# Linear attention into a two-layer ELU network on one core: a first load on another queue, a merged key-value product, and the stores of the last block

## The chip, the core and the metric

The kernel runs on one core of a Trainium2 chip. A core has five engines that run their own instruction streams and meet at semaphores: TensorE (PE, matrix products; its weight loads are shown apart as PEld), VectorE (DVE), ScalarE (ACT), GpSimd (POOL) and SyncE (SP). SP, ACT and POOL also start DMA transfers, each through a queue of its own. TensorE writes to PSUM, here eight banks of 128 x 512 floats, from where VectorE and ScalarE fetch results.

The metric is the device time in microseconds (us). The kernel before took 300.82 us (median of 4 runs, 300.44 to 300.91). The profiled execution is one more run.

## What is computed

Eight batches, eight heads, 576 positions, head size 64. The queries get a softmax over the head dimension, the keys one over the positions; the product of keys and values is a 64 x 64 matrix per head, by which the queries are multiplied. The result, 4608 tokens of 512, goes through two dense layers with ELU between them.

```python
def _attn_ref(q, k, v):
    q_s = np.exp(q - np.max(q, axis=-1, keepdims=True))
    q_s = q_s / (np.sum(q_s, axis=-1, keepdims=True) + 1e-09)
    k_s = np.exp(k - np.max(k, axis=2, keepdims=True))
    k_s = k_s / (np.sum(k_s, axis=2, keepdims=True) + 1e-09)
    kv = np.einsum('bhsd,bhse->bhde', k_s, v)
    return np.einsum('bhsd,bhde->bhse', q_s, kv)

def _moe_ref(x, w_in, w_out):          # x: 4608 x 512
    h = x @ w_in                       # 512 x 2048
    g = np.where(h > 0.0, h, np.exp(np.minimum(h, 0.0)) - 1.0)
    return g @ w_out                   # 2048 x 512
```

## The kernel before

**Units and blocks.** The attention works in 16 units `n`, two per batch; a unit is four heads of a batch. The dense layers work in nine blocks `j` of 512 tokens. Each block has a hidden phase (`hg`, eight groups `g` of two 128-row tiles, L550 to L591) and an output phase (`out_mm`, L593, in which four token groups `ts` of 128 gather their 16 products `jj` in a bank each, and `out_store`, L607). Batch 0 is worked off ahead of block 0. During block `j`'s output phase the attention of batch `j + 1` is slipped in between pieces of the output products.

**Steps of a unit.** Exp of q on ScalarE (L357), the sums and their reciprocal on VectorE (L363, L366), the scaling to half precision (L377), a transpose. For units 0 to 3 the transpose is TensorE's (`tp`, L424), for later ones a DMA's (L381). Exp of k (L397) and v cast to bfloat16 (L403 on GpSimd, L406 on VectorE for units 0 to 3). `kv` (L438) forms the key-value products on TensorE (L451), in 36 small matmuls for each unit it is given; the last column of v is all ones and gives the key sums. VectorE turns that into the matrix MBLK (L464 reciprocal, L469 two products). `ao` (L482) multiplies the queries by MBLK in two parts `x` (L492), and the result is copied to XT, the input of the dense layers, by ScalarE alone (`evac="act"`, L512) or half by ScalarE and half by VectorE (`evac="split"`, L504 and L508).

**Banks.** The eight banks are four pairs, `PS[0]` to `PS[3]`, named A, Bs, C and Dd by role and rotated from block to block. The output phase keeps its four sums in A and Bs; C and Dd are there for transposes, key-value products and attention products. The argument `ps` of `tp`, `kv` and `ao` says which pair.

**First loads.** `program` (L639) starts with four loads for q of units 0 and 1, two per unit (one per half of the heads, 288 KB each), listed as (unit, half). Those of unit 0 and the first of unit 1 are issued by SP, the second of unit 1 by GpSimd (L648). Behind it on GpSimd's queue follow k and v of units 0 and 1 (576 KB each), w_in in 16 pieces of 256 KB (four slices, `W1CUT`), and then w_out in five slices (`W2CUT`: jj 0-4, 4-8, 8-12, 12-14, 14-16) mixed with q, k and v of units 2 and 3, in the order of L688. Loads of later units are SP's (L304) and begin when the last w_out slice has landed.

**Order.** TensorE's instructions run in the order in which the program adds them. For ScalarE, VectorE, GpSimd and SP, `Sched.order` plays the program through with costs per instruction and assumed DMA times, and fixes each engine's order; `op.late` is added to the assumed landing of a load (L652). The waits themselves follow from what an instruction reads and writes.

**Block 0's output phase.** `plan` has 20 pieces, five w_out slices by four token groups: pieces 0 to 11 of four matmuls, 12 to 19 of two. `work` (L763) says after which piece a step of batch 1 comes: the transposes after pieces 6 and 9, unit 2's key-value product after 10 in C, unit 2's attention products after 12 (Dd) and 13 (C), unit 3's key-value product after 14 in Dd, its attention products after 16 (C) and, as `last`, after 17 (Dd). The local function `kv` (L748) also starts loads of k and v of the unit two further on. From block 1 on `kv` is called once for both units.

**Stores.** `out_store` copies a finished 128 x 512 sum to OSB on ScalarE (L613) and stores it in two halves `x`. All are issued by SP, save the second half of the very last sum, which ScalarE issues (L618).

Of the kernel before, what the change touches and what calls it, by code (L numbers as in the profile page):

```python
# [14 lines left out]
NBLK = B * S // BLK  # L15
# [236 lines left out]
class Gen:  # L252
# [386 lines left out]
    def program(self):  # L639
        S = self.S  # L640
        self.eslot = self.oslot = 0
        self.init()
        sp = gp = None
        for n, h in ((0, 0), (0, 1), (1, 0), (1, 1)):
            src = self.src["q"][0, 4 * h + 2 * n:4 * h + 2 * n + 2, :, :].rearrange(
                "f (p c) d -> (f p) (c d)", c=CH)
            dst = self.RQ[n][:, h, :, :].rearrange("p c d -> p (c d)")
            eng = "gp" if n * h else "sp"  # L648
            op = S.add(eng, 450 if eng == "sp" else 760, lambda e, src=src, dst=dst: e.dma_start(dst, src),  # L649
                       -90, W=[f"qR{n}h{h}"], dma=f"q{n}h{h}", nbytes=128 * 2304,  # L650
                       follow=gp if eng == "gp" else sp, tag=f"ld q{n}")
            op.late = 1300 if n == 0 else 1000 if eng == "sp" else 2000  # L652
            if eng == "gp":
                gp = op
            else:
                sp = op
        for n, t in ((0, "k"), (0, "v"), (1, "k"), (1, "v")):
            gp = self.load(n, t, "gp", -80, follow=gp)
            gp.late = 2200 if (n, t) != (1, "v") else 1650
        for s in range(len(W1CUT) - 1):  # L660
            gp = self.load_w1(s, -60, follow=gp)
        S.add("act", 1400, lambda e: e.activation(
            self.RZK[0][:, :], self.RZK[0][:, :], AF.Exp), -65, X=["RZK0"])
        self.spin(40, 0)
        self.q_part(0, -90)
        self.q_mul(0, -90, None)
        self.spin(9, 0, "expq0")
        self.spin(10, 0, "rec0")
        self.q_part(1, -85)
        self.q_mul(1, -85, None)  # L670
        self.k_part(0, -80, vconv="dve")
        self.tp(0, 3, -84)
        self.spin(16, 0)
        self.spin(6, 0, "rec1")
        self.spin(4, 0, "expk0")
        self.tp(1, 1, -78)
        self.kv([0], 2, -82)
        self.spin(5, 0)
        self.spin(4, 0, "rzk0")
        self.k_part(1, -81, vconv="dve", behind="M0")  # L680
        self.ao(0, 0, 0, -83, evac="split")
        self.spin(4, 6)
        self.kv([1], 1, -82)
        self.hg_mm(0, 0, 3, (0, 1))
        self.ao(1, 0, 0, -75, evac="split")
        self.hg_mm(0, 1, 2, (0, 1))
        self.ao_last(0, 1, -60)
        for what in (0, "2q", "3q", 1, "2k", "2v", 2, "3k", "3v", 3, 4):  # L688
            if isinstance(what, int):
                gp = self.load_w2(what, -50, follow=gp)  # L690
            else:
                gp = self.load(int(what[0]), what[1], "gp", -50, follow=gp)
        self.ldq, self.w2 = None, [gp]
        for op in S.ops:
            if op.dma and op.eng == "gp" and not op.late:
                op.late = 1800
        S.rel = self.pe

        def loads(n, ts, key):
            for t in ts:  # L700
                self.ldq = self.load(n, t, "sp", key, after=self.w2, follow=self.ldq)
                self.w2 = ()

        def elem_q(b, key, dmat="sp"):
            for n in (2 * b, 2 * b + 1):
                self.q_part(n, key)
                if b != 2:
                    self.q_mul(n, key, dmat)

        def elem_k(b, key, vconv="gp"):  # L710
            for n in (2 * b, 2 * b + 1):
                self.k_part(n, key, vconv)

        def convert(b, key):
            for n in (2 * b, 2 * b + 1):
                self.cvt(n, key)

        key = 0
        A, Bs, C, Dd = 3, 2, 1, 0
        for j in range(NBLK):  # L720
            order = [A, Bs, C, Dd]
            for g in range(8):
                self.hg(j, g, order[g % 4], key, j or g > 2,
                        (0, 1, 2, 3) if j or g > 1 else (2, 3))
                key += 1
                if (j, g) == (0, 0):
                    elem_q(1, 8, None)
                    elem_k(1, 8, "dve")
            if j == 1:
                S.rel = self.pe  # L730
                for n in (4, 5):
                    self.q_mul(n, key, "sp")
                convert(2, key)
            b = j + 1
            more = b + 1 < B
            work = {}
            k1 = key + 14
            if b < B:
                n0, n1 = 2 * b, 2 * b + 1
                S.slack = 3500 if j else 1500  # L740
                if more:
                    loads(n0 + 2, "q", key)
                    loads(n1 + 2, "q", key)
                    S.rel = self.pe
                    if j:
                        elem_q(b + 1, k1)

                def kv(units, ps=C, more=more):  # L748
                    self.kv(units, ps, key)
                    for n in units:  # L750
                        if more:
                            loads(n + 2, "kv", key)
                            self.k_part(n + 2, k1)

                def last(n1=n1, b=b, ps=C if j else Dd, more=more):
                    self.ao(n1, 1, ps, key, evac="act" if j else "split")
                    if more and b > 1:
                        convert(b + 1, k1)
                def ao(n, x, ps):
                    return lambda: self.ao(n, x, ps, key)  # L760

                if j == 0:
                    work = dict(zip((6, 9, 10, 12, 13, 14, 16, 17), (  # L763
                        lambda: self.tp(2, C, key), lambda: self.tp(3, Dd, key),
                        lambda: kv([2]), ao(2, 0, Dd), ao(2, 1, C),
                        lambda: kv([3], Dd), lambda: self.ao(3, 0, C, key, evac="split"), last)))
                else:
                    work = dict(zip((5, 11, 12, 13, 14) if j == 1 else (3, 6, 8, 9, 11), (
                        lambda: kv([n0, n1]), ao(n0, 0, Dd), ao(n0, 1, C), ao(n1, 0, Dd), last)))
            if j == 0:  # L770
                plan = [(ts, W2CUT[s], W2CUT[s + 1]) for s in range(5) for ts in range(4)]
            else:
                plan = [(ts + t, jj, jj + 4) for ts in (0, 2) for jj in range(0, 16, 4) for t in range(2)]
            if j == NBLK - 1:
                plan = plan[:8] + [(ts, jj, jj + 4) for ts in (2, 3) for jj in range(0, 16, 4)]
            bank = [2 * A, 2 * A + 1, 2 * Bs, 2 * Bs + 1]
            for k, (ts, jj0, jj1) in enumerate(plan):
                self.out_mm(j, ts, bank[ts], jj0, jj1, key)
                if jj1 == 16:
                    self.out_store(j, ts, bank[ts], key, last=(j, ts) == (NBLK - 1, 3))  # L780
                if k in work:
                    work[k]()
                key += 8 / len(plan)
            if j == 0:
                S.rel = self.pe
                elem_q(2, k1)
            A, Bs, C, Dd = Dd, C, A, Bs
# [32 lines left out]
```

## Time and profile before

| what | value |
|---|---|
| median of 4 runs | 300.82 us |
| profiled execution | 301.03 us |
| its span | 299.2 us |
| PE busy | 289.9 us (97%) |
| DVE, ACT, POOL busy | 153.7, 153.8, 123.4 us |
| DMA, first five slices of 7.5 us | 241, 392, 387, 389, 392 GB/s |
| hidden phase of block 0 in full swing | 19.19 to 32.01 us |
| output phase of block 0 | 32.01 to 50.35 us |
| last output copy on ScalarE | 295.55 us |

The span is the time from the first to the last instruction that the profiler shows; the rest of the execution's time, 1.83 us, lies around it. Times in the profile are from the span's start. "L599" is a line of the kernel. TensorE's clock was granted in full in every slice.

Landings of the first loads, from the views of the single tiles (issue and time from issue to landing, us):

| load | issued by | issue | to landing |
|---|---|---|---|
| q unit 0, half 0 | SP | 0.74 | 2.8 |
| q unit 0, half 1 | SP | 1.21 | 3.1 |
| q unit 1, half 0 | SP | 1.66 | 6.5 |
| q unit 1, half 1 | POOL | 1.27 | 5.6 |
| k unit 0 | POOL | 2.00 | 6.7 |
| v unit 0 | POOL | 2.71 | 7.5 |
| k unit 1 | POOL | 3.42 | 8.3 |
| v unit 1 | POOL | 4.12 | 9.1 |
| w_out slice 2 (jj 8-12) | POOL | 18.45 | 21.2 |
| k unit 3 | POOL | 19.2 | 22.0 |
| v unit 3 | POOL | 19.9 | 22.8 |
| w_out slice 3 (jj 12-14) | POOL | 20.6 | 23.4 |

### The profile page before, as it was taken

What the parts mean: (1) busy time and instruction counts of PE and PEld (TensorE: products, weight loads), DVE (VectorE), ACT (ScalarE), POOL (GpSimd) and SP (SyncE); (2) the same over time, 40 slices, a digit from 0 to 9 for tenths busy, and PEclk for the clock granted to TensorE, in tenths of its full rate; (3) what the DMA queues carried; (4) which work ended last, traced back from release to release, by engine and by line L of the source; (5) the groups of instructions that cost most, each with busy time, mean ns of one, the idle gap of its engine ahead of it and who ended that gap; (6) DMA issues with size and microseconds to landing.
All of it is one profiled execution on the core that took longest, in us unless ns stands there. A gap on an engine that the chain in (4) does not pass through costs nothing.

```text
span 299.2 us, 4561 instructions
## 1 busy us (share of the span) xinstructions
PE 289.9 (97%) x1926; PEld 238.1 (80%) x1926; DVE 153.7 (51%) x187; ACT 153.8 (51%) x183; POOL 123.4 (41%) x130
## 2 busy tenths in 40 slices
PE   6599999999999999999999999999999999999995
PEld 6478877888888888888888888888878888888883
DVE  5649862869537833684168606770662046105600
ACT  3745646872585465547455555545543355125411
POOL 8994300671177144723282228414550055005500
PEclk9999999999999999999999999999999999999999
DMA  7999988935994499029900992089002110230032
GB/s 241 392 387 389 392 274 278 360 138 72 295 275 132 130 369 198 0 64 360 270 2 8 386 244 58 2 263 265 9 0 57 45 41 2 47 75 18 2 71 70
DMA packets 36165, 49.98 MB, mean 167 GB/s; under 512 B 16496, under 2 KB 16496, under 8 KB 36144
## 3 DMA queue, kind: packets, MB, share of 16 engines
q1 hardware_dynamic: 30112, 34.97, 41.8%
q0 software_dynamic: 5952, 14.58, 15.3%
q8 instruction: 15, 0.25, 0.3%
q10 hardware_dynamic: 80, 0.13, 0.1%
q14 instruction: 6, 0.05, 0.0%
HBM read 36.70 MB, written 9.44 MB: 154 GB/s over the span
## 4 chain that ended last, share of the span: by engine, by line
PE 94%; DMA 2%; DVE 2%; ACT 1%; SPq 0%; issue 0%
PE PS L599 45%; PE PS L559 44%; PE PS L492 3%; DMA QR<-in_q_dram 2%; PE PS L451 2%; PE PS L424 1%; DVE QS L377 0%; DVE ZQ L363 0%; ACT QR L357 0%; SPq L649 0%; DVE XT L508 0%; DVE MBLK L469 0%; ACT OSB L613 0%; PE PS L524 0%; DVE RZQ L366 0%
## 5 line engine op out<-in xcount | busy, mean ns | idle before, releaser
L599 PE MATMUL PS<-W,GT 128*128 128x512 f32 x576 | 140.6, 393 | 0.0
L582 DVE SCALAR_TENSOR_TENSOR GT<-ESB,PS 128x1024 fp32r<-128x1024 f32 x69 | 84.1, 1221 | 109.5 <-POOL ESB L579 109.4
L559 PE MATMUL PS<-XT,W 128*128 128x512 f32 x576 | 132.7, 390 | 0.1
L559 PEld LDWEIGHTS PS<-XT,W 128*128 128x128 f32 x576 | 107.9, 188 | 22.8 <-DVE XT L508 0.2
L599 PEld LDWEIGHTS PS<-W,GT 128*128 128x128 f32 x576 | 105.9, 188 | 20.9 <-DMA W<-in_moe_w_out_dram 0.3
L579 POOL TENSOR_SCALAR ESB<-ESB 128x1024 f32<-128x1024 f32 x69 | 71.9, 1043 | 103.9 <-ACT ESB L574 103.7
L574 ACT ACTIVATE ESB<-PS 128x1024 f32<-128x1024 f32 x72 | 73.9, 1028 | 51.4 <-PE PS L559 51.4
L613 ACT ACTIVATE OSB<-PS 128x512 f32<-128x512 f32 x36 | 21.4, 599 | 61.6 <-PE PS L599 61.4
L403 POOL CAST VB<-VR 128x1152 bf16<-128x1152 f32 x12 | 16.3, 1354 | 46.2 <-DMA VR<-in_v_dram 46.2
L363 DVE TENSOR_REDUCE ZQ<-QR 128x18 f32<-128x1152 f32 (+1 forms) x17 | 21.7, 1278 | 7.2 <-ACT QR L357 7.2
L512 ACT ACTIVATE XT<-PS 128x640 fp32r<-128x640 f32 (+3 forms) x26 | 16.9, 651 | 14.4 <-PE PS L492 14.4
L377 DVE TENSOR_TENSOR QS<-QR,RZQ 128x1152 f16<-128x1152 f32 x16 | 21.7, 1368 | 0.4
L357 ACT ACTIVATE QR<-QR 128x1152 f32<-128x1152 f32 (+1 forms) x18 | 18.5, 1053 | 4.9 <-DMA QR<-in_q_dram 4.9
L397 ACT ACTIVATE KR<-KR 128x1152 bf16<-128x1152 f32 x16 | 18.5, 1155 | 2.9 <-DMA KR<-in_k_dram 2.8
L390 POOL CAST qsT<-QR 128x1152 fp32r<-128x1152 f16 x12 | 13.8, 1147 | 8.5 <-DMA QR<-QS 7.8
L492 PE MATMUL PS<-qsT,MBLK 128*128 128x320 f32 (+4 forms) x60 | 13.5, 307 | 0.2 <-DVE MBLK L469 0.2
L492 PEld LDWEIGHTS PS<-qsT,MBLK 128*128 128x128 f32 x60 | 11.2, 189 | 3.1 <-DVE MBLK L469 0.7
L545 PE MATMUL PS<-IDLE 128*128 128x128 f16 x98 | 8.0, 243 | 3.9 <-DVE RZQ L366 2.5
L545 PEld LDWEIGHTS PS<-IDLE 128*128 128x128 f16 x98 | 6.8, 110 | 4.8 <-DVE RZQ L366 2.9
L316 POOL DMA_DIRECT2D W<-in_moe_w_in_dram x16 | 10.4, 1372 | 0.0
L469 DVE TENSOR_TENSOR MBLK<-PS,RZK 64x128 fp32r<-64x128 f32 x32 | 9.3, 289 | 1.1
L327 POOL DMA_DIRECT2D W<-in_moe_w_out_dram x5 | 9.7, 2283 | 0.0
(31 smaller groups left out, 62.2 us busy)
## 6 DMA issues: line engine op xcount, KB each, us to landing
out_dram<-OSB SPq DMA_DIRECT2D x71, 128.0 KB, 2.5
QR<-in_q_dram SPq DMA_DIRECT2D x12, 576.0 KB, 7.9
KR<-in_k_dram SPq DMA_DIRECT2D x12, 576.0 KB, 5.9
VR<-in_v_dram SPq DMA_DIRECT2D x12, 576.0 KB, 6.7
W<-in_moe_w_in_dram POOLq DMA_DIRECT2D x16, 256.0 KB, 11.4
W<-in_moe_w_out_dram POOLq DMA_DIRECT2D x3, 1024.0 KB, 17.7
KR<-in_k_dram POOLq DMA_DIRECT2D x4, 576.0 KB, 13.3
VR<-in_v_dram POOLq DMA_DIRECT2D x4, 576.0 KB, 14.2
```

What stands on the lines that cost most here:

```text
L357: lambda e, part=part: e.activation(part, part, AF.Exp), key,
L363: S.add("dve", 1350 if n else 750, lambda e, z=z, src=src: e.tensor_reduce(z, src, AX.X, ALU.add), key, R=self.q_res(n) if n else [f"qR0h{ ...
L377: S.add("dve", 1400, lambda e: e.tensor_tensor(qso, raw[:, :, :, :], rz, ALU.mult), key, R=qR + [f"RZQ{i}"], W=[f"QS{al}"], low=True, tag= ...
L397: S.add("act", t_act(1152, False), lambda e: e.activation(ek[:, :, :, :].rearrange("p h c d -> p (h c d)"), flat, AF.Exp), key, X=[f"kR{i} ...
L492: return e.matmul(P[:, f * 512:f * 512 + n_], M[:, f, :], T[:, c0:c1, f * 64:f * 64 + 64], start=True, stop=True)
L512: S.add("act", t_act(2 * n_, True), lambda e: e.activation(dst, src, AF.Copy), key, W=names(0) + names(1), X=self.banks(ps), tag=f"evx{n}")
L559: last = e.matmul(P[:, t * 512:(t + 1) * 512], self.W1[:, kc, tt * 128:(tt + 1) * 128], self.XT[:, kc, rc:rc + BLK], start=(kc == 0), stop ...
L574: S.add("act", t_act(1024, True), lambda e: e.activation(esb[:, :], P[:, :], AF.Exp), key, W=[f"E{i}"], X=self.banks(ps), tag=f"exp{j}.{g}")
L579: S.add("gp", 1120, lambda e: e.tensor_scalar(esb[:, :], esb[:, :], 1.0, 0.0, ALU.min, ALU.max), key, X=[f"E{i}"], tag=f"min{j}.{g}", port ...
L582: S.add("dve", t_dve(1024), lambda e: e.scalar_tensor_tensor(gt, esb[:, :], -1.0, P[:, :], ALU.add, ALU.max), key, R=[f"E{i}"], W=gw, X=se ...
L599: last = e.matmul(dst, GT[:, jj, ts * 128:(ts + 1) * 128], self.W2[:, jj, :], start=(jj == 0), stop=(jj == 15))
L613: S.add("act", t_act(512, True), lambda e: e.activation(osb[:, :], src, AF.Copy), key, W=[f"O{i}0", f"O{i}1"], X=[f"b{bk}"], tag=f"evo{jb} ...
```

## The change

Three edits. The first half of unit 1's q is issued by GpSimd too, so that GpSimd's queue begins with both halves and SP issues only unit 0's; the planner's extra time for it is 2000 ns instead of 1000. In block 0's output phase one call of `kv` takes both units of batch 1, after piece 11 in C; unit 2's attention products follow after 14 (Dd) and 15 (C), unit 3's after 16 (Dd) and 17 (C). In the last block each of the four sums has its second half stored by ScalarE.

```diff
@@ program, first loads
-            eng = "gp" if n * h else "sp"
+            eng = "gp" if n else "sp"
...
-            op.late = 1300 if n == 0 else 1000 if eng == "sp" else 2000
+            op.late = 1300 if n == 0 else 2000
@@ program, steps of the attention within an output phase
-                def last(n1=n1, b=b, ps=C if j else Dd, more=more):
+                def last(n1=n1, b=b, ps=C, more=more):
                     self.ao(n1, 1, ps, key, evac="act" if j else "split")
...
                 if j == 0:
-                    work = dict(zip((6, 9, 10, 12, 13, 14, 16, 17), (
-                        lambda: self.tp(2, C, key), lambda: self.tp(3, Dd, key),
-                        lambda: kv([2]), ao(2, 0, Dd), ao(2, 1, C),
-                        lambda: kv([3], Dd), lambda: self.ao(3, 0, C, key, evac="split"), last)))
+                    work = dict(zip((6, 9, 11, 14, 15, 16, 17), (
+                        lambda: self.tp(2, C, key), lambda: self.tp(3, Dd, key), lambda: kv([2, 3]),
+                        ao(2, 0, Dd), ao(2, 1, C), lambda: self.ao(3, 0, Dd, key, evac="split"), last)))
@@ program, stores
-                    self.out_store(j, ts, bank[ts], key, last=(j, ts) == (NBLK - 1, 3))
+                    self.out_store(j, ts, bank[ts], key, last=j == NBLK - 1)
```

## The prediction

> **What bounds the kernel now.** I read the chain of work that ended last first, in order of time. From 16.2 us to 295.5 us it is TensorE with hardly a break, so a part of the change counts only where it takes TensorE work out, or where it moves the few moments at which TensorE waits.
>
> ```profile
> 1.66 6.51 DMA QR<-in_q_dram
> ...
> 9.48 1.36 DVE ZQ L363
> ...
> 19.19 12.82 PE PS L559 x56
> 32.01 6.34 PE PS L599 x28
> 38.35 0.52 PE PS L424 x9
> 38.87 2.99 PE PS L599 x12
> ...
> 43.36 0.41 PE PS L451 x36
> 43.78 1.59 PE PS L599 x6
> ...
> 46.83 0.42 PE PS L451 x35
> 47.25 1.13 PE PS L599 x4
> ...
> 70.40 0.70 PE PS L451 x68
> 71.11 5.68 PE PS L599 x24
> ```
>
> Columns: start, duration, what (both in us). Before 16 us the chain hangs on the third q load (unit 1, heads' first half), issued by SP at 1.66 and landing at 8.17. From 19 us on the price of a 128x512 matmul is 12.82 / 56 = 0.229 us in the hidden layer and 6.34 / 28 = 0.226 in the output layer. At that price the 12 of 38.87 need 2.72, so 0.27 of their 2.99 was lost, and after each key-value product the row is long too: 1.59 - 6 x 0.2265 = 0.23 and 1.13 - 4 x 0.2265 = 0.22.
>
> Next the timeline of block 0's output phase and the waits, for those 0.27 us:
>
> ```profile
> 39.72 1.70 PEld L599 LDWEIGHTS PS<-W,GT 128*128 128x128 f32 x8 [0.30 <-DMA W<-in_moe_w_out_dram]
> 42.72 0.77 DVE L406 CAST VB<-VR 128x1152 bf16<-128x1152 f32 x1 [1.62 <-DMA VR<-in_v_dram]
> ```
>
> The bracket is the idle time before it and its cause. TensorE stood for the third slice of w_out (rows jj 8 to 12). By the tile view of W that slice was issued on GpSimd's queue at 18.45 and landed 21.2 us later, at 39.7. The DMA row is full until then: 241, 392, 387, 389, 392 GB/s in the first five slices. **So the first 40 us have two limits of nearly equal length: the attention chain of unit 1, and GpSimd's stream of loads.** TensorE came to the slice 0.3 us before its data.
>
> **Part 1: unit 1's q on GpSimd's queue.** SP loses one issue (0.43 us), GpSimd gains one (0.73). q half 0 takes the slot at 1.27 that half 1 had, half 1 the slot at 2.00, and k0, v0, k1, v1, the triangle for the identity (4.93), 16 pieces of w_in and the w_out, q, k, v loads behind them are each issued one slot, 0.7 us, later. Identity: needed by the transpose at 7.50, ready about 6.0 instead of 5.3; covered. GpSimd's last issue starts at 21.3 and its first minimum at 25.9; covered.
>
> When does q1 land? Half 1 on GpSimd took 5.6 us (1.27 to 6.9), half 0 on SP 6.5 (1.66 to 8.17). The load in the 2.00 slot was k0, with twice the bytes, and landed at 8.7. 288 KB at the 1.5 us per 576 KB by which k0, v0, k1, v1 follow each other is 0.75 us. So half 1 lands between 6.9 + 0.3 = 7.2 and, at worst, 8.7 - 0.75 = 7.95. I take 7.2, since SP's half no longer takes turns with it. The Exp of half 0 (0.63) is then done before half 1 lands, so VectorE's sum starts at 7.2 + 0.65 = 7.9 instead of 9.48: **1.6 us earlier** (0.8 at worst). Behind it all follows alike: sum 1.36, reciprocal 0.28, product 1.37, v0's cast 0.79 (v0 is there at 10.2, needed at 10.9).
>
> What is late next? The w_in pieces: by the tile view the last piece of the second slice is issued at 8.9 and lands 11.3 later, at 20.2. TensorE starts the group that needs it at 19.19 + 8 x 0.229 = 21.0. So at most 0.8 of the 1.6 gets past there. Then comes the w_out slice at 39.7, for which TensorE already waits: nothing gets past that. **The attention chain's gain is worth 0 by itself**; it only makes the wait longer (0.3 to about 1.1 us). What counts is whether the slice lands at 39.7 or not.
>
> Here the Trainium skill has a rule that speaks against any effect ("DMA: Bandwidth & Descriptors", section "Issuing engines are not separate DMA queues"): DMAs run on the same 16 engines whoever starts them, and a second issuer saves only issue time. By the rule the bytes ahead of the slice are the same and the shift is 0. The trace, which can be read by queue in a window, qualifies it. From 4.0 to 5.5 us:
>
> ```profile
> DMA packets 165, 0.44 MB, mean 292 GB/s; under 512 B 21, under 2 KB 21, under 8 KB 165
> ...
> q0 software_dynamic: 59, 0.21, 52.4%
> q1 hardware_dynamic: 106, 0.23, 46.3%
> ```
>
> q0 is GpSimd's, q1 SP's. While GpSimd's stream got going, SP's queue moved more than half of the bytes. From 4 to 8 us both moved 325 GB/s, from 8 to 12 GpSimd alone 400. Read one way, SP fills gaps that GpSimd cannot yet fill: without it 0.23 MB / 0.4 = 0.58 us of the stream are lost, and with the issue slot 0.73 on top at worst 1.3 us. Read the other way, the mixing costs: (400 - 325) GB/s x 4 us = 0.30 MB, 0.75 us that one queue alone would win. Ends: -0.75 and +1.3. I take 0, the rule's value, because both readings rest on the same window and the landings of k0 to v1 stand 1.5 us apart (393 GB/s) directly behind it, with 10 us of issues in hand.
>
> **Part 2: one key-value product for units 2 and 3.** Removed: two stays of 0.41 and 0.42 with 0.23 and 0.22 lost behind them, 1.28 us. Added: one stay like that of the later blocks, 0.70 (two units, 70.40) with 5.68 - 24 x 0.2265 = 0.24 behind, 0.94. **Gain 0.34 us**, on the path, behind the w_out slice, so nothing swallows it. Does the later stay wait for more? It stands after piece 11 of the plan: the slice at about 40.05, 16 matmuls (3.63) and the transposes with what they cost (0.52 + ~0.1) give 44.3. It needs unit 3's k (Exp over at 42.4) and v (cast over at 42.72 + 0.77 = 43.5): 0.8 us of cover, which would also bear a stream later by 0.7. Behind it the next output piece needs the fourth slice (20.6 + 23.4 = 44.0): there at 45.2. Both units' reciprocals and products (0.17 + 0.61 each) are over 1.7 us after the stay; unit 2's first attention product comes 3 pieces, 1.6 us, after it and needs only its own half of that. The four attention products then stand one 0.45 us piece apart in two alternating banks, each needing a copy of 0.4 to 0.65 on ScalarE, among output copies of 0.60. Laid out one after the other with these durations, the banks come free 0.2 to 0.5 us before TensorE wants them. The last copy into XT ended at 50.11, with the next block's weights at 50.16: no cover there. Ends for this: 0 to +0.6 (one output copy ahead of the XT copy). Taken: 0, since two pieces (0.92 us) stand between as now. Loads of unit 5's k and v no longer wait for a second stay; they go out about 47 instead of 52.9 and push block 0's stores back, which nobody needs for 20 us.
>
> **Part 3: stores of the last block.** Three stores go from SP to ScalarE, each issue about 0.55 (the row of the one store there). ScalarE copies at 287.4, 288.3, 291.9 and 295.5, 0.6 each: the copy at 288.3 slips by about 0.3, and its bank is not used again. The last copy and its two stores, one per queue at 296.2, stay as they are. SP's waits at the end take 17 to 28 ns each and lie within the last store's 2.2 to 2.6 us of landing. Worth 0; ends -0.1 and +0.1.
>
> **Sum.** 0 - 0.34 + 0 = -0.34 us. The profiled execution took 301.03 (span 299.2 and 1.83 around it), so it would be 300.69; it lies 0.21 above the median of the runs shown, 300.82, to which I refer the forecast: **300.5 us**, -0.11%. What a measurement of this kernel can tell from no change is about 0.2%, 0.6 us: 300.2 to 301.4.
>
> **Rivals.**
> *Stream earlier*: without SP's turns GpSimd's loads run at 400 GB/s from 4 us on, the slice lands up to 0.75 earlier and TensorE, itself early now, takes it: -0.34 - 0.75 = -1.1, 299.7. For it: 325 against 400 GB/s, and TensorE would be there. Against: GpSimd's own share in that window was small for want of work of its own. It takes 0.3 us to get past 0.2%.
> *Stream later (the slower side)*: the gaps at 4 to 5.5 us stay empty and each load is issued a slot later, so TensorE waits at the w_out slice; price 0.58 to 1.3, from a shift of 0.34 on slower than before; with the middle, 0.95, +0.6: 301.4. For it: the wait exists already, so every 0.1 us shows. Against: the issues run far ahead of the landings.
> *Order*: VectorE's and ScalarE's orders come from a planner in the kernel, which sees other due times; an output copy put ahead of an XT copy costs 0.6 at the end of block 0 and perhaps again in block 1: +0.3 to +0.9, 301.4.
> *Nothing new*: that q1 doesn't land earlier is possible (8.17 to 7.95) and changes nothing in the sum.
>
> **Chances.** Forecast 0.40, stream earlier 0.28, stream later 0.21, order 0.11. The forecast's own range is 300.3 to 300.7. Faster by over 0.2%: nearly all of the second, 0.28. Slower by over 0.2%: half of the third and most of the fourth, 0.21. Within: 0.51. Range for 8 in 10: from 299.6 (the earlier stream in full) to 301.6 (the later one short of its worst).
>
> **What would show it.** Step 1: VectorE's sum of unit 1 near 7.9. Step 2: idle time before the weights at the third w_out slice grown from 0.30 to about 1, and its landing still 39.7 +- 0.3; another landing time says which rival it is. Step 3: one row of about 0.70 at L451 near 44.3 with no wait on VB, and hidden block 1 starting near 50.0 instead of 50.35. Step 4: the same 3.7 us from the last output copy's start to the end. I am wrong if the landing moves, if the stay waits for v, or if TensorE stands for XT at 50 us.

## The result and the profile after

The changed kernel takes 299.73 us (median of 34 runs, 299.15 to 301.58), the kernel before beside it 300.79 (53 runs). The ratio is 0.9963, 95% interval 0.9953 to 0.9973: faster by 0.37%, about 1.1 us. The forecast of 300.5 was short of that; its range held it, and the rival "stream earlier" (299.7) came closest. Executions differ by the clock that TensorE was granted, as a mean over the span: 30 of the 34 of the changed kernel had 0.997 or more of full speed (median 299.62), the other four 0.993 or 0.994 (300.94); for the 53 beside them the clocks are not on record.

The profiled execution has a span of 297.5 us, against 299.2. First the chain that ended last in the changed kernel, in order of time (start, duration in us, what):

```profile
19.01 19.61 DMA W<-in_moe_w_out_dram
38.62 0.04 issue
38.66 2.11 PE PS L599 x8
40.77 0.52 PE PS L424 x9
41.29 1.88 PE PS L599 x8
43.17 0.70 PE PS L451 x67
43.88 1.60 PE PS L599 x6
45.47 0.29 PE PS L492 x2
...
46.93 0.30 PE PS L492 x2
...
47.92 0.92 PE PS L599 x4
48.85 1.36 PE PS L559 x6
```

The same places in the kernel before:

```profile
41.86 0.52 PE PS L424 x9
...
48.38 0.36 PE PS L492 x2
...
50.35 4.86 PE PS L559 x21
```

TensorE's work of the first 38 us has left the chain: TensorE's part now begins behind the load of the third w_out slice, which landed at 38.62 instead of 39.7. From unit 3's transposes (L424 at 41.86 and at 40.77) on there is one key-value row of 0.70 instead of two. Next the timeline around the two places that the forecast spoke of:

```profile
7.48 1.34 DVE L363 TENSOR_REDUCE ZQ<-QR 128x18 f32<-128x1152 f32 x1
...
38.66 1.69 PEld L599 LDWEIGHTS PS<-W,GT 128*128 128x128 f32 x8 [1.05 <-DMA W<-in_moe_w_out_dram]
...
41.66 0.77 DVE L406 CAST VB<-VR 128x1152 bf16<-128x1152 f32 x1 [1.71 <-DMA VR<-in_v_dram]
43.10 0.67 PEld L451 LDWEIGHTS PS<-VB,KR 64*64 64x64 bf16 x72 [0.35 <-issue]
```

The sum of unit 1's q starts at 7.48 instead of 9.48. The idle time before the weights at the slice has grown from 0.30 to 1.05 us: TensorE is early there, and the data are not. The key-value product waits for nothing but its own queue; v was cast by 42.4.

Where the 1.7 us of the two spans come from, place by place:

| stretch | before | after | difference |
|---|---|---|---|
| start to unit 3's transposes (L424) | 41.86 | 40.77 | -1.09 |
| from there to block 1's hidden phase | 8.49 | 8.08 | -0.41 |
| block 1's hidden phase | 14.61 | 14.51 | -0.10 |
| rest, to the last output copy (L613) | 230.59 | 230.58 | -0.01 |
| last output copy to the end | 3.65 | 3.56 | -0.09 |

Each row is worked out from starts in the chain and the timeline: 50.35 - 41.86 = 8.49 and 48.85 - 40.77 = 8.08, for instance. The first row is one pair of executions; the experiments show how far it scatters.

### The profile page after: what moved, and what is told of

Read it like the earlier page. It is cut to its first block, busy times and chain, and to the rows that moved or that the text cites. A ratio compares the mean times of both kernels' runs of the same rounds, so it can differ in the third digit from the quotient of the medians.

```text
span 297.5 us, 4561 instructions
## 1 busy us (share of the span) xinstructions
PE 290.0 (97%) x1926; PEld 238.8 (80%) x1926; DVE 153.6 (52%) x187; ACT 153.6 (52%) x183; POOL 123.9 (42%) x131
## 4 chain that ended last, share of the span: by engine, by line
PE 86%; DMA 7%; POOL 6%; issue 0%; ACT 0%; POOLq 0%
PE PS L599 42%; PE PS L559 39%; DMA W<-in_moe_w_out_dram 7%; POOL W L316 3%; PE PS L492 3%; PE PS L451 2%; POOL W L327 0%; POOL KR L304 0%; POOL QR L304 0%; POOL QR L649 0%; POOL VR L304 0%; ACT OSB L613 0%; PE PS L424 0%; POOL ID L628 0%; POOLq L628 0%
## 5 line engine op out<-in xcount | busy, mean ns | idle before, releaser
L613 ACT ACTIVATE OSB<-PS 128x512 f32<-128x512 f32 x36 | 21.3, 601 | 60.2 <-PE PS L599 60.0
L316 POOL DMA_DIRECT2D W<-in_moe_w_in_dram x16 | 10.4, 1320 | 0.0
L545 PEld LDWEIGHTS PS<-IDLE 128*128 128x128 f16 x98 | 7.4, 118 | 2.2 <-DVE IDLE L631 1.1
```

The lines of the kernel that those rows point to most:

```text
L316: "gp", ISSUE["gp"], lambda e, kc=kc: e.dma_start(self.W1[:, kc, sl], w[kc, :, :, sl]), key,
L613: S.add("act", t_act(512, True), lambda e: e.activation(osb[:, :], src, AF.Copy), key, W=[f"O{i}0", f"O{i}1"], X=[f"b{bk}"], tag=f"evo{jb} ...
```

## The experiments

Each kernel is compared with the kernel before, run beside it on the same chip; the intervals of the ratios are 95%.

### One part of the change at a time

q alone (`e1_q_only`):

```diff
-            eng = "gp" if n * h else "sp"
+            eng = "gp" if n else "sp"
...
-            op.late = 1300 if n == 0 else 1000 if eng == "sp" else 2000
+            op.late = 1300 if n == 0 else 2000
```

> The kernel before with the first edit alone: both halves of unit 1's q on GpSimd's queue. Theory (the stream of loads lands earlier): the third w_out slice lands about 38.7 instead of 39.7 us and TensorE still waits for it, by 0.3 to 1 us; time down by 0.7 to 1.1 us, ratio 0.9965 to 0.9977. Rival 'chance' (the late start of the stream in the profile of before was that execution's, not the kernel's): landing 39.5 or later as often as not, ratio 0.999 to 1.001. Rival 'chain' (the attention chain's 1.9 us is what counts): no wait for w_out at all, ratio below 0.995.

Measured: 300.12 us, ratio 0.9978 (0.9959 to 0.9998), some 0.66 us. TensorE waits for the slice, which starts it at 38.82:

```profile
38.82 1.69 PEld L599 LDWEIGHTS PS<-W,GT 128*128 128x128 f32 x8 [1.26 <-DMA W<-in_moe_w_out_dram]
```

In this profile the gain comes by way of the slice. "Chance" as the whole story falls: the interval lies below 1, barely. How the gain divides between this edit and the next the ratios do not say; their intervals overlap.

The merged product alone (`e2_kv_only`: the edit of `last` and of `work` for block 0):

```diff
-                def last(n1=n1, b=b, ps=C if j else Dd, more=more):
+                def last(n1=n1, b=b, ps=C, more=more):
...
-                    work = dict(zip((6, 9, 10, 12, 13, 14, 16, 17), (
-                        lambda: self.tp(2, C, key), lambda: self.tp(3, Dd, key),
-                        lambda: kv([2]), ao(2, 0, Dd), ao(2, 1, C),
-                        lambda: kv([3], Dd), lambda: self.ao(3, 0, C, key, evac="split"), last)))
+                    work = dict(zip((6, 9, 11, 14, 15, 16, 17), (
+                        lambda: self.tp(2, C, key), lambda: self.tp(3, Dd, key), lambda: kv([2, 3]),
+                        ao(2, 0, Dd), ao(2, 1, C), lambda: self.ao(3, 0, Dd, key, evac="split"), last)))
```

> The kernel before with the second edit alone: one key-value product for units 2 and 3. Theory: the slice lands at 39.7 as before, one stay of 0.7 in place of two of 0.41, time down by 0.34 us, ratio 0.9989. Rival 'chance': the whole difference of the changed kernel sits here, ratio 0.9963. A third possibility, that the merged stay waits for v of unit 3: ratio 1.000 or above.

Measured: 300.37 us, 0.9983 (0.9960 to 1.0005). The interval doesn't tell 0.9989 from 1, but the profile does, since the stretch behind unit 3's transposes depends on nothing at the start. The chain of this kernel:

```profile
41.39 0.52 PE PS L424 x9
41.91 1.88 PE PS L599 x8
43.79 0.70 PE PS L451 x67
44.49 1.59 PE PS L599 x6
...
49.47 2.54 PE PS L559 x11
```

49.47 - 41.39 = 8.08 us. The same stretch took 8.48 to 8.50 in all six profiles with two stays (before, e1, e3, e5, e6 and r1, the second look at before) and 8.07 to 8.09 in the six with one and no wait for v (after, e2, e7, e9, r3 and r2, the second look at after). **The merge is worth 0.41 us, each time.**

This kernel starts as before does, and in its profile TensorE does not wait for the slice: the slice had landed at 39.1, and TensorE came to it at about 39.5 (four products behind the 38.60 of its chain). That chain runs back to SP's load of unit 1's q, which was summed at 8.86. So here the attention chain set the pace, not the slice.

The stores alone (`e3_stores_only`):

```diff
-                    self.out_store(j, ts, bank[ts], key, last=(j, ts) == (NBLK - 1, 3))
+                    self.out_store(j, ts, bank[ts], key, last=j == NBLK - 1)
```

> The kernel before with the third edit alone: second halves of the last block's stores issued by ScalarE. Every theory: ratio 0.9995 to 1.0005, and from the last output copy's start to the span's end 3.6 us as before. Its start is that of before, so its profile also says whether the late landings at the start come again: theory, unit 1's q half 0 lands near 8.2 and the third w_out slice near 39.7.

Measured: 300.49 us, 0.9993 (0.9969 to 1.0018); last output copy at 294.71, end at 298.3, 3.6 us. No effect that can be seen. The landings at the start did not come again as they were: the sum of unit 1's q began at 8.57 (9.48 in the first profile of before) and the slice's matmuls could start at 38.91 (39.72). The start of this kernel scatters from one execution to the next.

### Is the slice the limit?

The slice earlier, on top of the changed kernel (`e4_after_w2_first`, and `e8_after_w2_first_again` with more runs):

```diff
-        for what in (0, "2q", "3q", 1, "2k", "2v", 2, "3k", "3v", 3, 4):
+        for what in (0, "2q", "3q", 1, 2, "2k", "2v", "3k", "3v", 3, 4):
```

> The changed kernel with the third w_out slice issued before k and v of unit 2 instead of behind them. Theory: in the changed kernel TensorE waits for this slice (0.6 us of matmul time lost, 1.05 us before the weights); with the slice about 3 us earlier that goes, until the merged key-value product waits for unit 3's v, 0.7 us of cover: 0.6 us faster than the changed kernel, ratio to before 0.9943. Rival 'chain' (the attention chain alone made the gain, the slice is no limit): as the changed kernel, 0.9963.

> The same kernel as e4_after_w2_first, once more with more runs. Theory: again 1.4 to 2.4 us faster than before, ratio 0.992 to 0.9955, TensorE without a wait for w_out and stopped by v of unit 3 for under 0.6 us.

Measured: 299.41 us, 0.9930 (0.9895 to 0.9965), and 299.46 us, 0.9922 (0.9891 to 0.9954). No wait for w_out is left; TensorE is stopped by unit 3's v. The timeline of e4:

```profile
41.36 0.77 DVE L406 CAST VB<-VR 128x1152 bf16<-128x1152 f32 x1 [1.62 <-DMA VR<-in_v_dram]
42.18 0.67 PEld L451 LDWEIGHTS PS<-VB,KR 64*64 64x64 bf16 x72 [0.57 <-DVE VB L406]
```

The first bracket is VectorE's wait for v, the second TensorE's for the cast of v: the same stream of loads is the limit again, at a later load. In the profiles block 1's hidden phase starts at 47.93 (e4) and 48.67 (e8), against 48.85. This version beats the kernel before; against the changed kernel it leads in both medians, but the intervals of the ratios overlap.

The slice later (`e7_after_w2_later`), 1.5 us of loads further back:

```diff
-        for what in (0, "2q", "3q", 1, "2k", "2v", 2, "3k", "3v", 3, 4):
+        for what in (0, "2q", "3q", 1, "2k", "2v", "3k", 2, "3v", 3, 4):
```

> The changed kernel with the third w_out slice one load further back, behind k of unit 3: it lands 1.5 us later, near 40.4 us. Theory (in the changed kernel the attention chain is early and the slice sets the time): every microsecond shows, the weights wait about 2.5 us instead of 1.05, 1.5 us slower than the changed kernel, ratio to before 1.001 (0.9995 to 1.0025). Rival 'chain': no more than 0.5 us slower than the changed kernel, 0.998 or less.

Measured: 0.9992 (0.9977 to 1.0007), just below the expected range of 0.9995 to 1.0025. Its chain:

```profile
19.49 20.53 DMA W<-in_moe_w_out_dram
40.03 0.04 issue
40.07 2.11 PE PS L599 x8
...
50.25 1.86 PE PS L559 x8
```

The slice lands 1.4 us later than in the changed kernel (40.03 against 38.62), and block 1's hidden phase starts 1.4 later. In the ratios it is 0.9992 - 0.9963, 0.9 us, less than the profiles' 1.4. The clock can account for that: 18 of the 21 executions of e7 had 0.997 or more, but only 14 of the 49 of before beside them, and among these e7 took 301.25 us and before 300.84: there e7 is the slower one. More than the 0.5 us of "chain" it is: in the changed kernel a later slice costs time.

The slice earlier on top of the kernel before (`e5_before_w2_first`, the same diff as e4 on the other kernel):

> The kernel before with the third w_out slice issued before k and v of unit 2. Theory (before has two limits of nearly equal length, the attention chain and the slice): TensorE comes to that place no earlier than now, so only the 0.3 us of waiting can go: ratio 0.999 (0.998 to 1.000), a third or less of what the same edit gave on top of the changed kernel (0.9930 / 0.9963 = 0.9967). Rival (the slice's landing alone sets the time): as much as there, 0.9967 or less.

Measured: 0.9987 (0.9963 to 1.0010), as expected of two limits of nearly equal length. The profile shows the other one at work. The sum of unit 1's q:

```profile
10.14 1.35 DVE L363 TENSOR_REDUCE ZQ<-QR 128x18 f32<-128x1152 f32 x1 [2.61 <-ACT QR L357]
```

Here SP's load of unit 1's half 0 came so late that the sum began at 10.14. TensorE never waited for w_out and still came to block 1 only at 51.54. TensorE passed the slice's place at about 41.2, later than the 39.7 at which before's slice landed, so in this execution the attention chain would have set the end with the slice in its old place too. My forecast had ruled that out, but the late load is not all of it. The profile's row of TensorE's granted clock, in tenths over 40 slices of 7.5 us, is not full here:

```profile
PEclk9989999999999999999999999999999999999999
```

In short windows the clock is half of full speed from 14.3 to 17.7 us; two attention products take 1.22 us there and 0.74 in before. Unit 1's transposes start 0.65 us later than in before (13.24 against 12.59), by the load; block 0's hidden phase is in full swing 1.41 us later (20.60 against 19.19). The other 0.76 arises where the clock was half.

### Why does the start cost time?

I now thought that SP's loads and GpSimd's, in flight together, cost rate. `e6_all_q_sp` puts more of SP's beside GpSimd's:

```diff
-            eng = "gp" if n * h else "sp"
+            eng = "sp"
```

> The kernel before with all four first q loads on SP, so that GpSimd's queue starts with k of unit 0. Theory 'mixing' (the loss at the start comes while SP's and GpSimd's loads are in flight together): more bytes of SP's are under way beside GpSimd's, so the mean rate from 4 to 8 us stays near 325 GB/s or falls (400 and up would refute it), v of unit 1 lands at 13.2 or later against 12.3 to 12.9 with one queue, ratio 0.998 to 1.002. Rival 'half loads' (GpSimd's small first load is what is slow): rate from 4 to 8 us as in the changed kernel, 365 or more, v of unit 1 before 13.0, ratio below 0.998.

Measured: 303.64 us, 1.0064 (1.0045 to 1.0082), slower by 1.9 us, outside the range of either theory. The rate from 4 to 8 us is 301 GB/s, as "mixing" had it, but the time goes another way: the sum of unit 1's q,

```profile
11.12 1.35 DVE L363 TENSOR_REDUCE ZQ<-QR 128x18 f32<-128x1152 f32 x1 [3.61 <-ACT QR L357]
```

begins at 11.12 and TensorE doesn't wait for w_out at all. Both halves were issued in SP's queue by 2.6 us, and the second landed at 10.4. Here too the clock fell to half, from 12.9 to 16.2 us:

```profile
12.83 1.24 PE L545 MATMUL PS<-IDLE 128*128 128x128 f16 x10 [3.69 <-DVE RZQ L366]
```

These ten products took 0.73 us in before. Unit 1's transposes are 1.64 us later than in before, by the load, and the hidden phase in full swing is 2.27 later.

How the two queues share can be read in the kernel before, in the DMA views (packets, MB, share of the 16 engines' time; q0 is GpSimd's queue, q1 SP's). From 5 to 5.5 us:

```profile
q1 hardware_dynamic: 51, 0.10, 58.0%
q0 software_dynamic: 16, 0.06, 43.4%
```

and from 6 to 7:

```profile
q0 software_dynamic: 75, 0.31, 92.1%
q1 hardware_dynamic: 21, 0.04, 10.9%
```

At 6 us SP's queue had 27 packets left, and the last of them took 2 us to get through: the tail of SP's load comes late beside GpSimd's stream. That SP's queue as such is served last is not shown. It had the larger share at 5 us, and in e6, with more of SP's loads waiting, the two had 53.8% and 53.5% from 6.5 to 7.

Then the opposite, no load of SP's at the start (`e9_all_q_gp`, on the changed kernel):

```diff
-            eng = "gp" if n else "sp"
+            eng = "gp"
```

> The changed kernel with all four first q loads on GpSimd's queue, so that no load of SP's is ever in flight beside them. Theory 'mixing': from 4 to 8 us the rate is 370 GB/s or more, as high as in the quietest start of the changed kernel (380). But nothing moves before GpSimd's first bytes at about 3.6 us, where SP had moved 0.4 to 0.5 MB by then: the third w_out slice lands about 1.2 us later than in the changed kernel (near 39.9), TensorE waits for it, ratio to before 0.999 to 1.002. Rival 'slow start of GpSimd's queue' (its first loads run at 300 to 345 GB/s whatever SP does): rate from 4 to 8 us below 345, slice at 40.5 or later, ratio above 1.002.

Measured: 0.9991 (0.9966 to 1.0017), inside the range of "mixing". The DMA view from 4 to 8 us:

```profile
DMA packets 286, 1.08 MB, mean 271 GB/s; under 512 B 51, under 2 KB 51, under 8 KB 286
...
q0 software_dynamic: 286, 1.08, 93.1%
```

271 GB/s, the lowest of all, with nothing of SP's in flight. Mixing is not needed for a low rate. Two of the rival's three signs came, the rate below 345 and the slice late (TensorE could start there at 40.91), but not the third, a ratio above 1.002. To see whether it is the order of the loads or chance, three starts on one chip, no edits beyond those above:

> The kernel before once more, for the start of its loads on the same chip as the next two. If the rate from 4 to 8 us belongs to how the first loads are queued: 300 to 325 GB/s, third w_out slice at 39.0 to 39.8 us. If it is chance of the execution, it can be anything from 270 to 380.

> The changed kernel once more. If the queueing decides: 330 to 380 GB/s from 4 to 8 us, third w_out slice at 38.6 to 39.0, TensorE waits for it, and 8.08 us from unit 3's transposes to the next hidden phase (8.49 before). If chance decides, no order between this and the other two.

> All four first q loads on GpSimd, once more. e9_all_q_gp gave 271 GB/s from 4 to 8 us with no load of SP's in flight, against the theory that SP's loads beside GpSimd's are what costs. If that is how this queueing starts: 250 to 300 again. If it was chance: 340 or more, and the theory of mixing stands again.

Measured from 4 to 8 us: 343, 326 and 317 GB/s. Before and after have changed places, so the rate in that window is chance to a good part. And in this pair of executions the edit of q made no difference up to unit 3's transposes: they start at 41.33 in both. A piece of w_in landed late in both, and the 0.23 us by which before was ahead behind it were lost in a wait for the slice (idle 0.37 us, to 39.22). The chain of before,

```profile
5.73 9.73 DMA W<-in_moe_w_in_dram
15.46 0.25 issue
15.71 1.16 PE PS L559 x4
```

and of the changed kernel:

```profile
6.29 9.40 DMA W<-in_moe_w_in_dram
15.70 0.25 issue
15.94 1.16 PE PS L559 x4
```

What was left of the gain in this pair is 49.83 - 49.40 = 0.43 us, the merge. By time: 0.9987 (0.9951 to 1.0022) for before against itself, 0.9920 (0.9869 to 0.9972) for the changed kernel from four runs, and 1.0025 (0.9975 to 1.0076) with all q on GpSimd. The 0.9920 is more than this pair explains. All four executions of the changed kernel had the full clock, and 10 of the 13 of before beside them had not; against the other three it is 299.96 to 300.84 us.

What does go with the queueing is unit 1's q. Start of its sum on VectorE, us, by who issued what:

| unit 1's q | starts in the profiles |
|---|---|
| one half on SP (before, e2, e3, e5, r1) | 9.48, 8.86, 8.57, 10.14, 7.88 |
| both on GpSimd (after, e1, e4, e7, e8, r2) | 7.48, 7.43, 7.46, 7.88, 8.23, 7.96 |
| both on SP (e6) | 11.12 |
| both on GpSimd, behind unit 0's (e9, r3) | 9.28, 8.62 |

The means of the first two rows are 8.99 and 7.74: 1.25 us earlier, and steadier.

**The clock goes with it.** On the chip of e1 to e4, before took 300.35 us in the 39 executions with a mean clock of 0.997 or more, 301.62 in the 17 with 0.992 to 0.994, and 302.89 in the five below that. One stretch of 3.4 us at half clock, as in e5 and e9, gives a mean of 0.994; two, as in r3, give 0.989. Such executions are rarer where GpSimd issues both halves of unit 1's q: 7 of 31 on that chip (e1, e4) against 41 of 104 with one half on SP (before, e2, e3); on the chip of e5 to e8 3 of 30 (e7, e8) against 42 of 62 (before, e5), and all 17 of e6. At 0.997 or more, medians in us (number of executions):

| kernel | this | before beside it | difference |
|---|---|---|---|
| e1, q alone | 300.04 (16) | 300.35 (39) | -0.31 |
| e2, merge alone | 299.77 (11) | 300.35 (39) | -0.58 |
| e3, stores alone | 300.21 (13) | 300.35 (39) | -0.14 |
| e4, slice earlier | 299.20 (8) | 300.35 (39) | -1.15 |
| e8, the same again | 299.46 (9) | 300.84 (14) | -1.38 |
| e7, slice later | 301.25 (18) | 300.84 (14) | +0.41 |
| e5, slice earlier on before | 300.29 (6) | 300.84 (14) | -0.55 |
| e9, all q on GpSimd | 301.30 (7) | 300.75 (6) | +0.55 |

The groups are small, and half a microsecond is not certain in the last two rows.

What takes the clock down is open. TensorE had stood idle for 2.69 us in e5 and 3.69 in e6 shortly before, but for 2.12 in before without such a stretch, and in e9 no gap near it was longer than 0.89. No run tried it.

## Why the prediction was right and where not

**Unit 1's q.** Right. Forecast: sum at 7.9, 1.6 us earlier; measured 7.48, 2.0 earlier, and 1.25 earlier in the mean of the profiles. The half in the 2.00 slot landed 4.5 us after issue, 6.5 against the 7.2 that I took.

**"The attention chain's gain is worth 0 by itself."** Right for the execution that I had, too strong for the kernel. The wait at the slice grew to 1.05 as forecast ("about 1"). But e2 and e5 show executions of before's start in which TensorE came to the slice after it had landed: there the chain, not the slice, set the end. I read the landing of one load of SP's (6.5 us) as a fixed number; it scattered from 4.9 to 7.2.

**The stream of loads, "I take 0".** This is the step that failed: with the chain's gain at 0 as well, the sum had nothing for the edit of q. I had both ends (-0.75 and +1.3) and a rule for the middle, that it doesn't matter who issues. By e1's ratio this edit is worth about 0.66 us (0.06 to 1.2) over many executions. The 1.09 us of the two profiles are more than the edit's share, for the first profile of before was the latest of its kind. Unit 3's transposes started at 41.86, 41.39, 41.02 and 41.33 in before, e2, e3 and r1, and at 40.77, 40.94 and 41.33 in after, e1 and r2: 0.4 us between the means, and e1 gained 0.31 at the full clock. Part of the rest can be the stretches at half clock, for which the prediction has no term at all.

My reading behind the rival, that the mixing of queues costs 75 GB/s, doesn't hold either (e9, r1 against r2): the rival gave nearly the right time by luck, with a mechanism that the runs don't bear out. What they show in its place are three loads of which any can be the last: unit 1's q, the first pieces of w_in, the third w_out slice. The edit makes the first of them earlier and steadier. Whether it also moves the slice by itself stays open: by the views of W it landed at 39.7, 39.1, 38.9 and 39.2 in before, e2, e3 and r1, and at 38.6, 38.8 and 39.2 in after, e1 and r2.

**The merged product.** Right in mechanism, 0.41 measured for 0.34 in the sum. One stay with its loss is 0.94 as taken. The other 0.07 us, for which the sum had no term, are nearly all in unit 3's first attention product: its row is 0.36 in before (at 48.38) and 0.30 after (at 46.93). The wait for v did not come (0.8 us of cover forecast, v cast at 42.4 for a stay at 43.1). The XT copy, for which I had no cover to offer, came early enough: block 1's hidden phase, in which 0.10 us had been lost, took 14.51.

**Stores.** Right: nothing that can be told from 0 (0.9993, and 3.56 to 3.6 us at the end for 3.65).

The order that the planner gives to the engines changed in block 1 (sums and Exps of units 4 and 5 stand elsewhere), and cost nothing: the rest of the kernel took 230.58 us for 230.59.

## What to carry to other kernels

Before an edit at the start of a kernel is costed, look at more than one execution: here three loads arrive within about a microsecond of need, and which one ends last differs from run to run, so one profile names one limit and hides two. Look at the granted clock of each execution too, before two medians are compared: here one step of it goes with 1.3 us, as much as the whole gain. In this kernel the load that the first chain of work hangs on did best at the head of GpSimd's queue, better than on SP beside it and better than behind two others. Small matmul groups between large ones are worth merging where the data allow it: here each key-value group cost about 0.23 us beyond its own work, and one of 0.70 us replaced two of 0.41 and 0.42.

## What the hardware showed unexpectedly

A 288 KB load of q issued by SP at 1.66 us, with GpSimd's loads beside it, took 4.9 to 7.2 us to land in six profiles, and a second one behind it 8.2 (e6). With both halves on GpSimd they took 3.8 to 5.5 in six. GpSimd's half beside an SP half was slow as well, 4.6 to 6.4, so it is not SP's load alone that suffers.

The rate of the first loads from 4 to 8 us varied between 271 and 380 GB/s over the executions and was 388 to 404 in the four microseconds after it, save with every q load on GpSimd (358 and 373). Why it varies is open and was not tried further.

TensorE's clock fell to half for about 3.4 us within the first 21 us of some executions (e5, e6, e9, and twice in r3), and how often it did so changed with the queue of one load: 42 of 62 executions against 3 of 30 on one chip.
